# One store per 128 output rows, one DMA transposition each for q, k and exp(C), looser gates and a new instruction order in a fused Nyström attention and feed-forward kernel

## The chip, the cores and the metric

The kernel runs on one core of a Trainium2 chip. The metric is the time of one execution on the device in microseconds (us), as the median of several executions. The kernel before takes 248.0 us as the median of three runs (247.69, 248.0 and 253.92). One further execution was profiled; its own time was 247.08 us, and all durations below come from that one. The engines are called PE (TensorE, matmuls), PEld (its weight loads), DVE (VectorE), ACT (ScalarE), POOL (GpSimd) and SP (SyncE, which here only issues DMAs).

## The reference

The reference is an attention by landmarks followed by a feed-forward layer. q, k and v have 8 batches, 8 heads, 576 tokens and 64 values per head, all fp32. It is cut here to what matters:

```python
m, scale = 32, 1 / sqrt(64)
q_lm = q.reshape(B, H, 32, 18, 64).mean(axis=3)       # 32 landmarks, each the mean of 18 tokens
k_lm = k.reshape(B, H, 32, 18, 64).mean(axis=3)
A  = softmax(scale * q    @ k_lm.T)                   # 576 x 32
Bm = softmax(scale * q_lm @ k_lm.T)                   # 32 x 32
C  = softmax(scale * q_lm @ k.T)                      # 32 x 576
Z  = Bm.T / (norm_1(Bm) * norm_inf(Bm) + 1e-6)
for _ in range(6): Z = 2 * Z - Z @ Bm @ Z
x  = A @ Z @ C @ v                                    # heads side by side: 4608 x 512
h  = x @ w_in                                         # 4608 x 2048
out = (h * sigmoid(h)) @ w_out                        # 4608 x 512, fp32
```

## The kernel before, in words

The kernel works through the 8 batches, and several batches are in flight at once. The 8 heads of a batch are two groups g of four. A token has the number 18·l + j, where l is one of 32 landmarks and j one of 18 places; j is split into 9 pairs, so that j = 2·jp + c. After the transposition the two parities c lie on different halves of the partitions.

For each batch the work is this. POOL issues loads that cast to bf16 (`ld1` for k, `ld0` for q, three pieces `ldv` for v). q and k are transposed to `qT`: for batches 0 to 2 by TensorE, 128x128 at a time (`tr`, line 515, with copies `trc` behind them), for batches 3 to 7 by DMA from SP (`xt`, line 539), one DMA for each of q, k and each group g, so four of 9 blocks per batch. DVE adds the 18 places up to landmark sums (`lra` to `lrd`, line 575). PE transposes these sums (`ltr`), multiplies them (`sb`) and the rest of the chain makes Z (`ns`, `nsd`, `fb`). `A` and `C` are the two score products (each 16 tiled matmuls for both groups), `Ax` and `Cx` their exponentials on ACT, `ct` the transposition of exp(C) (by TensorE for batches 0 and 1, by DMA from SP for the others, line 814, one DMA of 6 blocks per group). `cv` multiplies exp(C) with v, `zt` with Z, and `m` with w_in, so that the first feed-forward product is done from the 128-deep `m`. DVE normalises exp(A) into `etn` (line 761), a tile of 128 partitions and 576 columns per group; its columns stand in the order c, j pair, l.

Layer 1 of a batch is 16 pieces `h` of two matmuls with 512 columns of `etn` (8 of the 9 pairs), followed by `g`, the silu on ACT (line 913), and 2 pieces `hx` of 16 matmuls with 64 columns (the ninth pair), followed by `gx`. The tokens of `hx` from four batches are collected in one tile. Layer 2 takes 256 tokens at a time by Strassen's scheme: seven products `p1` to `p7` of 8 matmuls with 256 columns, the sums `ss` on DVE before them, and copies and additions (`c`, `u`) behind them. Each 128 rows of the result lie in one of six `ost` buffers and are stored from there by four DMAs of 32 rows (`os`, line 978), from SP, at the end from SP and ACT.

The order of everything is written out by hand in one long string (`SEQUENCE`): each word is one operation, a word `*n` stands for n filler matmuls of zeros (`warm`), and `/DVE` or `/ACT` names the engine that takes a copy. Each engine executes its own words in this order, so an instruction that waits holds up all behind it on its engine. Buffers of PSUM are given out in this order too. Further dependencies are added as gates, so that transpositions and loads keep apart: a transposition `xt` of batch b waits for the second of the three v loads of its batch (line 534), the loads of batch b+1 wait for one transposition of batch b (the third in the list `xts`) and for the first `ct` of the batch before (lines 1098 to 1100), and each load waits for the eighth load before it (in `load`, line 360).

Of the kernel before, what the change touches and what calls it, by code (L numbers as in the profile page):

```python
# [8 lines left out]
BF = mybir.dt.bfloat16  # L9
# [10 lines left out]
ldk ld11.0 const ident k0cACT k0cDVE k0 *15 lms100.0 tr15.0 tr10.0 trc10.0/DVE lms106.0 lms1012.0  # L20
*6 lms110.0 lms116.0 tr114.0 lms1112.0 lmc1.0/DVE ld00.0 *6 lms000.0 tr05.0 tr00.0 trc05.0/ACT
trc114.0/ACT ltr1.0 lmT1.0/ACT trc00.0/DVE tr19.0 trc19.0/DVE trc15.0/DVE lms006.0 ld01.0
lms0012.0 lms010.0 lms016.0 lms0112.0 ld0.1 ld1.1 ldv2.0 ldv0.0 wi0b1 ldv1.0 wi0b0 tr09.0 tr014.0
lmc0.0/DVE *1 ltr0.0 lmT0.0/ACT *6 sb.0 pb.0 trc014.0/DVE trc09.0/DVE A.0 Ax01.0 Ax00.0 Ax10.0
Ax11.0 *5 C.0 Cx01.0 Cx10.0 Cx11.0 Cx00.0 pbs.0 pbr.0 bmx.0 bmt.0 csb.0 n1.0 nrm.0 tr09.1 lms000.1
lms006.1 S10.0 lms0012.1 lms010.1 bbd.0 trc09.1/DVE stz.0 f0.0 stf0.0 stf1.0 fb00.0 lms016.1
Ln10.0 S00.0 Ln00.0 fb01.0 lms0112.1 lmc0.1/DVE S01.0 ns00.0 nsd00.0 Ln01.0 S11.0 ns01.0 Ln11.0
nsd01.0 fb11.0 ctm00.0 ctc00.0/DVE tr05.1 trc05.1/ACT tr00.1 trc00.1/ACT Rs1.0 Rs0.0 ns11.0
nsd11.0 fb10.0 fb21.0 tr19.1 trc19.1/DVE ltr0.1 lms100.1 lms106.1 ns10.0 nsd10.0 lms1012.1 tr014.1
lms110.1 lms116.1 trc014.1/DVE ns21.0 tr114.1 lmT0.1/ACT wi1a wi0a wi1b1 wi1b0 wi3b0 wi3a  # L30
lms1112.1 lmc1.1/ACT tr10.1 trc10.1/ACT tr15.1 *2 ltr1.1 lmT1.1/ACT fb20.0 nsd21.0 etn1.0
trc15.1/DVE ns20.0 fb31.0 *3 ns31.0 ctm10.0 trc114.1/ACT etn0.0 nsd31.0 sb.1 pb.1 *1 A.1 Ax01.1
Ax00.1 nsd20.0 fb30.0 pbs.1 wrc.0 *1 ns30.0 nsd30.0 ctc10.0/DVE fb40.0 pbr.1 fb41.0 bmx.1 bmt.1
wi3b1 Ax11.1 Ax10.1 *5 C.1 Cx00.1 Cx11.1 Cx01.1 *1 ns40.0 nsd40.0 ns41.0 nsd41.0 fb50.0 fb51.0
cv0.0 cv1.0 wc.0 S01.1 Ln01.1 ns50.0 nsd50.0 *2 ns51.0 bbd.1 nsd51.0 zbd.0 S11.1 Ln11.1 S00.1
Ln00.1 wi2b0 wi2b1 wi2a ldv0.1 ldv1.1 *5 zt.0 ztc.0/DVE S10.1 ctm00.1 ctc00.1/DVE Rs0.1 Ln10.1
Cx10.1 *2 m1.0 mc11.0/ACT mc10.0/DVE m0.0 f0.1 mc01.0/DVE mc00.0/ACT *1 ctm10.1 ctc10.1/DVE Rs1.1
csb.1 *1 h4.0 n1.1 m3.0 nrm.1 stz.1 stf0.1 mc31.0/DVE fb00.1 g4.0 mc30.0/DVE h2.0 g2.0 h6.0 g6.0
h0.0 g0.0 h3.0 ns00.1 wrc.1 nsd00.1 fb10.1 h5.0 g5.0 m2.0 mc21.0/ACT mc20.0/DVE *1 h13.0 g13.0
ns10.1 nsd10.1 fb20.1 h15.0 hx0.0 g15.0 ns20.1 nsd20.1 fb30.1 h9.0 g9.0 h11.0 g11.0 etn0.1 ns30.1  # L40
nsd30.1 fb40.1 hx8.0 gx8.0 g3.0 h8.0 h12.0 g12.0 etn1.1 ns40.1 nsd40.1 fb50.1 gx0.0 h10.0 g10.0
ld1.2 tr15.2 trc15.2/DVE h14.0 g14.0 ns50.1 nsd50.1 zbd.1 ldv2.1 cv0.1 wc.1 tr114.2 trc114.2/DVE
tr19.2 trc19.2/DVE zt.1 g8.0 ztc.1/ACT tr10.2 trc10.2/DVE lra1.2 h7.0 g7.0 m3.1 mc31.1/ACT
mc30.1/ACT m1.1 mc11.1/DVE mc10.1/ACT h1.0 g1.0 ld0.2 tr00.2 lrb1.2 tr09.2 tr014.2 trc014.2/DVE
tr05.2 trc05.2/DVE trc09.2/DVE lrc1.2 trc00.2/ACT h12.1 g12.1 h7.1 g7.1 h15.1 m2.1 mc20.1/ACT m0.1
# [199 lines left out]
def kernel(  # L245
# [917 lines left out]
```

## Time and profile before

| what | value |
|---|---|
| median of three runs | 248.0 us |
| the profiled execution: its own time, its span from first to last instruction | 247.08 us, 245.4 us |
| mean granted TensorE clock | 0.985 |
| PE busy | 233.3 us (95% of the span) |
| PEld, DVE, ACT, POOL busy | 165.8, 180.0, 180.8, 36.7 us |
| HBM read and written | 36.70 MB, 9.44 MB |
| stores (`out_dram<-ost`) on SP and on ACT | 133 and 19 |
| DMA transpositions on SP (`qT<-qk`, `ct<-ce`) | 20 and 12 |

The span is what the engines were seen to do; 1.7 us of the execution's time lie around it. Busy shares are averages over stages that are bound by different things, so the prediction reads the stretches where PE was not busy or not at full clock, and the rows that tell what it waited for. A matmul's duration in the profile includes its way through the array, so two that follow each other overlap; what a matmul costs PE is the distance from its start to the start of the next one.

### The profile page before, as it was taken

Reading aid. Unit: us, or ns where it says so; the run is one execution under the profiler, and the core shown is the slowest. Engines: PE = TensorE matmul, PEld = TensorE weight load, DVE = VectorE, ACT = ScalarE, POOL = GpSimd, SP = SyncE. Lnnn points to the kernel's source line nnn. Section 1 sums busy time; section 2 is a strip of 40 time slices with the busy share of each in tenths; the row PEclk is TensorE's granted clock in tenths of the full one; section 3 lists DMA queues with packets and bytes.
Section 4 is the critical chain, followed back from the end, with each engine's and each line's share of the span. In section 5 each row is a group of like instructions: output and inputs, shape, how many; then the busy total and the mean of one; then the engine's idle time right before and its main releaser. Section 6 shows DMA issues by size and latency. Waiting matters only on the chain.

```text
span 245.4 us, 7471 instructions
## 1 busy us (share of the span) xinstructions
PE 233.3 (95%) x2948; PEld 165.8 (68%) x2948; DVE 180.0 (73%) x503; ACT 180.8 (74%) x432; POOL 36.7 (15%) x62
## 2 busy tenths in 40 slices
PE   7999999999999999199999999999999999999992
PEld 5986464457867556067878754777876765789882
DVE  2589889789998591489798968938899475348752
ACT  3299999988989998159746699999779788634100
POOL 8346713000050040000130060000000000000000
PEclk9999999999999999769999999999999999999999
DMA  6999999999999999793999999985414421012343
GB/s 160 207 203 197 206 207 206 210 205 204 132 177 220 202 137 178 185 194 98 136 190 171 167 185 239 190 145 136 108 47 117 121 52 39 1 43 77 88 119 109
DMA packets 55876, 36.84 MB, mean 150 GB/s; under 512 B 36640, under 2 KB 47392, under 8 KB 55840
## 3 DMA queue, kind: packets, MB, share of 16 engines
q0 software_dynamic: 15120, 18.06, 45.1%
q1 hardware_dynamic: 39808, 17.35, 34.9%
q10 hardware_dynamic: 912, 0.95, 1.4%
q8 instruction: 23, 0.38, 0.6%
q14 instruction: 13, 0.11, 0.1%
HBM read 36.70 MB, written 9.44 MB: 188 GB/s over the span
## 4 chain that ended last, share of the span: by engine, by line
PE 78%; ACT 7%; DMA 7%; SPq 3%; issue 1%; DVE 1%; ACTq 0%; DVEq 0%
PE ps L325 74%; DMA qT<-qk 6%; PE ps L515 3%; SPq L539 2%; ACT gm L913 2%; DMA gm<-in_k_dram 1%; ACT L913 1%; SPq L814 1%; ACT L1116 1%; ACT gx L936 1%; ACT m L335 1%; PE ps L802 1%; DVE red L575 1%; ACT pb L641 1%; ACT et L742 0%
## 5 line engine op out<-in xcount | busy, mean ns | idle before, releaser
L913 ACT ACTIVATE gm<-ps 128x512 f16<-128x512 f32 x128 | 68.7, 621 | 15.0 <-PE ps L325 14.3
L325 PE MATMUL ps<-etn,m 128*128 128x512 bf16 (+1 forms) x512 | 73.5, 289 | 0.2
L325 PEld LDWEIGHTS <-gm 128*128 128x128 f16 x512 | 48.6, 98 | 12.5 <-issue 1.3
L325 PE MATMUL ps<-w_out_sb,gm 128*128 128x256 f16 (+1 forms) x392 | 53.0, 281 | 0.0
L325 PEld LDWEIGHTS <-ss 128*128 128x128 f16 x408 | 39.5, 99 | 9.8 <-issue 1.8
L325 PEld LDWEIGHTS <-m 128*128 128x128 bf16 x512 | 31.5, 98 | 20.8 <-issue 3.2
L325 PE MATMUL ps<-wt,ss 128*128 128x256 f16 x272 | 35.5, 276 | 0.2
L1036 DVE TENSOR_TENSOR ost<-ost,ps 128x256 f32<-128x256 f32 x51 | 20.9, 416 | 13.4 <-PE ps L325 7.4
L335 ACT COPY ost<-ps 128x256 f32<-128x256 f32 (+1 forms) x45 | 17.2, 388 | 10.9 <-PE ps L325 10.6
L335 ACT CAST m<-ps 128x512 bf16<-128x512 f32 x36 | 19.4, 612 | 1.1 <-PE ps L325 0.8
L337 DVE CAST m<-ps 128x512 bf16<-128x512 f32 x28 | 18.3, 685 | 2.3 <-PE ps L325 1.9
L710 DVE SCALAR_TENSOR_TENSOR st<-st,ps 128x128 bf16<-128x128 bf16 (+2 forms) x54 | 13.6, 257 | 8.5 <-PE ps L325 5.5
L407 POOL DMA_DIRECT2D v<-in_v_dram x24 | 14.0, 590 | 30.8 <-DMA qT<-qk 13.6
L325 PE MATMUL ps<-w_out_sb,ss 128*128 128x256 f16 x136 | 17.5, 273 | 0.0
L325 PE MATMUL ps<-wt,gm 128*128 128x256 f16 x120 | 15.5, 272 | 0.0
L575 DVE TENSOR_TENSOR red<-qT 128x1024 f16<-128x1024 bf16 x12 | 8.3, 689 | 9.4 <-DMA qT<-qk 9.2
L685 DVE TENSOR_TENSOR fb<-st,hmask 128x256 bf16<-128x256 bf16 (+1 forms) x54 | 14.4, 271 | 0.8
L752 ACT ACTIVATE ln<-ps 128x288 f32<-128x288 f32 x32 | 12.4, 423 | 2.7 <-PE ps L325 2.4
L787 ACT ACTIVATE ce<-ps 128x288 bf16<-128x288 f32 x32 | 13.0, 424 | 1.7 <-PE ps L325 1.6
L1001 DVE TENSOR_TENSOR ss<-gm 128x1024 f16<-128x1024 f16 x15 | 10.2, 686 | 5.2 <-ACT gm L913 5.2
L742 ACT ACTIVATE et<-ps 128x288 bf16<-128x288 f32 x32 | 11.1, 423 | 3.6 <-PE ps L325 3.6
L337 DVE COPY ost<-ps 128x256 f32<-128x256 f32 x25 | 10.5, 420 | 3.2 <-PE ps L325 3.0
(93 smaller groups left out, 332.0 us busy)
## 6 DMA issues: line engine op xcount, KB each, us to landing
out_dram<-ost SPq DMA_DIRECT2D x126, 64.0 KB, 2.1
v<-in_v_dram POOLq DMA_DIRECT2D x24, 192.0 KB, 10.0
qk<-in_q_dram POOLq DMA_DIRECT2D x7, 576.0 KB, 10.6
qk<-in_k_dram POOLq DMA_DIRECT2D x7, 576.0 KB, 9.2
w_out_sb<-in_moe_w_out_dram POOLq DMA_DIRECT2D x4, 512.0 KB, 15.1
w_in_sb<-in_moe_w_in_dram POOLq DMA_DIRECT2D x8, 128.0 KB, 7.2
w_in_sb<-in_moe_w_in_dram POOLq DMA_DIRECT2D x4, 256.0 KB, 9.0
out_dram<-ost ACTq DMA_DIRECT2D x10, 64.0 KB, 1.7
```

The source lines that it names most:

```text
L325: nc.tensor.matmul(out=out_ap, lhsT=lhsT, rhs=rhs, start=start, stop=stop, skip_group_check=True)
L335: nc.scalar.copy(out=out, in_=in_)
L337: nc.vector.tensor_copy(out=out, in_=in_)
L407: lambda e, a=a: nc.gpsimd.dma_start(out=v_r[b % 2][a * L:(a + 1) * L, :, :], in_=v[b].rearrange("h (l a x) d -> a l h (x d)", l=L, a=VA)[ ...
L575: lambda e: nc.vector.tensor_tensor(out=o_, in0=a_, in1=b_, op=OP.add),
L685: nc.vector.tensor_tensor(out=fb[it % 2][:, g0:g1], in0=bc(sr[it % 3][:, g0:g1, 0:L], 4, 2), in1=bc(hmask, n, 1), op=OP.mult), [o], 14.5 + ...
L710: nc.vector.scalar_tensor_tensor(out=s2[:, g0:g1, lo:SW], in0=s[:, g0:g1, lo:SW], scalar=2.0, in1=ps[:, 0:NG * SW].rearrange("p (g x) -> p ...
L742: lambda e, g=g, et=et, c=c: nc.scalar.activation(out=et[:, c], in_=bank(me["A"], 2 * g + c)[:, 0:HS], func=AF.Exp, scale=sc / J),
L752: lambda e, g=g, c=c, ln=ln: nc.scalar.activation(out=ln[:, c], in_=bank(me["S", g, c])[:, 0:HS], func=AF.Ln),
L787: nc.scalar.activation(out=ce[:, :, 0:VP].rearrange("p (i c) (a l) -> p c a i l", c=2, a=VA)[:, c], in_=bank(me["C"], 2 * g + c)[:, 0:HS]. ...
L913: lambda e, dc=dc, cell=cell: nc.scalar.activation(out=gm[:, dc, :], in_=bank(cell["o"]), func=AF.Silu),
L1036: nc.vector.tensor_tensor(out=out_, in0=x, in1=y, op=OP.add)
```

## The change

The change touches the order and the layout of the columns of `etn`, and with it the tokens that a store writes.

- `etn` is written in the order c, l, j pair instead of c, j pair, l. The instruction still runs over j and then l, so its output steps by 9 elements (18 bytes) from one element to the next. `h` reads runs of 8 elements with one left out between runs. `hx` reads the ninth element of each run, with the two halves c next to each other in its order: neighbours in its stream lie 288 elements apart.
- By that, 128 result rows are 16 landmarks times 8 places of one parity, and one DMA stores them. The last pair goes out as 64 rows per batch.
- q and k are transposed by one DMA of 18 blocks each (not one per group), exp(C) by one of 12 blocks.
- Gates: a transposition waits for the first v load, not the second; the loads of the next batch wait for the first transposition in the list; the dependency on the eighth load before is dropped from the plan (the eight semaphores of the POOL queue still make an eighth load wait); three of the four preparations of w_out for Strassen's scheme and the first silus lose a dependency.
- `A` and `C` are two operations each, one per group, with two PSUM banks each instead of four.
- The order string is another one throughout, with 84 fillers instead of 64 and, on ACT, 13 changes of the activation table after the first instead of 11.

Batches 0 to 2 are transposed by TensorE in both versions; what is new is where these transpositions stand in the order.

```diff
 SEQUENCE = """
-ldk ld11.0 const ident k0cACT k0cDVE k0 *15 lms100.0 tr15.0 tr10.0 trc10.0/DVE lms106.0 lms1012.0
+const ldk ld11.0 ident ld00.0 ld01.0 ld0.1 k0cDVE k0cACT ld1.1 fold k0 *18 lms100.0 lms106.0
...
-ce_r = ring(smp, [128, VI, 128], BF, "ce", 2)
-ct_r = ring(smp, [128, VI, 128], BF, "ct", 2)
+ce_t = smp.tile([128, NG, VI, 128], BF, tag="ce", name="ce")
+ct_t = smp.tile([128, NG, VI, 128], BF, tag="ct", name="ct")
+ce_r, ct_r = [ce_t[:, g] for g in range(NG)], [ct_t[:, g] for g in range(NG)]
...
     def load(name, prio, us, issue, emit, deps=(), after=()):
         d = list(deps) + list(after)
-        if len(swdge) >= 8:
-            d.append((swdge[-8], None))
...
-            gate = v_ops[b][-2:-1]
+            gate = v_ops[b][:1]
             for t in (1, 0):
-                for g in range(NG):
-                    qt_ops[t, g] = [A(
-                        f"xt{t}{g}.{b}", [("SP", 1.38)],
-                        lambda e, t=t, g=g: nc.sync.dma_start_transpose(
-                            out=qT[:, t, g], in_=qk[:, t, g].rearrange("p j d -> p (j d)")),
-                        [qk_ops[b, t, g]] + use + gate, p0 + 5, lag=XLAG)]
...
+                o = A(f"xt{t}.{b}", [("SP", 1.8)],
+                      lambda e, t=t: nc.sync.dma_start_transpose(
+                          out=qT[:, t].rearrange("p g j x -> p (g j) x"),
+                          in_=qk[:, t].rearrange("p g j d -> p (g j d)")),
+                      [qk_ops[b, t, g] for g in range(NG)] + use + gate, p0 + 5, lag=XLAG)
...
             def etm(e, g=g, et=et, ln=ln):
-                nc.vector.tensor_tensor(out=etn[:, g, :], in0=et.rearrange("p c x -> p (c x)"),
-                                        in1=ln.rearrange("p c x -> p (c x)"), op=OP.mult)
+                nc.vector.tensor_tensor(
+                    out=etn[:, g, :].rearrange("p (c l j) -> p c j l", c=2, l=L),
+                    in0=et.rearrange("p c (j l) -> p c j l", l=L),
+                    in1=ln.rearrange("p c (j l) -> p c j l", l=L), op=OP.mult)
...
-                ct_ops[g] = [A(f"ct{g}.{b}", [("SP", 1.38)], lambda e, ce=ce, ct=ct:
...
+                after = v_ops.get(b + 1, [])[:1]
+                ct_ops[0] = ct_ops[1] = me["cts"] = [A(
+                    f"ct0.{b}", [("SP", 1.5)], lambda e: nc.sync.dma_start_transpose(
+                        out=ct_t.rearrange("p g i x -> p (g i) x"),
+                        in_=ce_t.rearrange("p g i x -> p (g i x)")),
+                    me["csum", 0] + me["csum", 1] + [prev.get("cv")] + after, p0 + 20, lag=XLAG)]
...
             def hm(e, dc=dc, cell=cell):
                 ps = bank(cell["o"])
                 for g in range(NG):
-                    mm(ps.rearrange("p (c x) -> p c x", c=2),
-                       m_sb[:, g, dc * 128:(dc + 1) * 128], etc[:, g, :, 0:256],
+                    mm(ps.rearrange("p (c l j) -> p c l j", c=2, l=L),
+                       m_sb[:, g, dc * 128:(dc + 1) * 128], etc[:, g, :, :, 0:JP - 1],
                        start=(g == 0), stop=(g == 1))
...
                         for g in range(NG):
-                            mm(ps[:, d].rearrange("p (c x) -> p c x", c=2),
+                            mm(ps[:, d].rearrange("p (l c) -> p l c", c=2),
                                m_sb[:, g, (d0 + d) * 128:(d0 + d + 1) * 128],
-                               etc[:, g, :, 256:288], start=(g == 0), stop=(g == 1))
+                               etc[:, g, :, :, JP - 1].rearrange("p c l -> p l c"),
+                               start=(g == 0), stop=(g == 1))
...
-    def store(e, t, place, m, cols=slice(0, DMODEL)):
-        b, j = place[m]
-        {"SP": nc.sync, "ACT": nc.scalar}[e].dma_start(
-            out=out[b * S:(b + 1) * S, cols].rearrange("(l j) n -> j l n", j=J)[j],
-            in_=t[L * m:L * m + L, cols])
+    def store(e, t, place, cols=slice(0, DMODEL)):
+        b, c, h = place
+        q = {"SP": nc.sync, "ACT": nc.scalar}[e]
+        if h is not None:
+            return q.dma_start(out=out[b * S:(b + 1) * S, cols].rearrange(
+                "(l j c) n -> c l j n", c=2, j=JP)[c, L // 2 * h:L // 2 * (h + 1), 0:JP - 1],
+                in_=t[:, cols])
+        r = [q.dma_start(out=out[x * S:(x + 1) * S, cols].rearrange(
+            "(l j) n -> l j n", j=J)[:, J - 2:J], in_=t[64 * n:64 * n + 64, cols])
+            for n, x in enumerate((b, b + 1)) if c is None or n == c]
+        return r[0]
...
     def later_loads(b):
         p = last[b - 2]
-        gate = last[b - 1].get("xts", [])[-2:-1]
+        gate = last[b - 1].get("xts", [])[:1]
         if b - 2 >= NCT:
             gate = gate + last[b - 2]["cts"][:1]
```

More of the change, by code (lines that the diff above doesn't have):

```diff
@@ L26 @@
[L26 to L31, printed above, removed]
@@ L502, in attn @@
         qt_ops = {}
-        use = [prev2[x] for x in ("A", "C") if x in prev2]
+        use = [prev2[x, g] for x in "AC" for g in range(NG) if (x, g) in prev2]
         if on_pe:
@@ L742, in attn @@
                       lambda e, g=g, et=et, c=c: nc.scalar.activation(
-                          out=et[:, c], in_=bank(me["A"], 2 * g + c)[:, 0:HS], func=AF.Exp,
+                          out=et[:, c], in_=bank(me["A", g], c)[:, 0:HS], func=AF.Exp,
                           scale=sc / J),
-                      [me["A"], prev.get(f"etn{g}")], p0 + 21 + g, table="exp",
-                      group=grp).reads(me["A"], 2 * g + c)
+                      [me["A", g], prev.get(f"etn{g}")], p0 + 21 + g, table="exp",
+                      group=grp).reads(me["A", g], c)
                 me["S", g, c] = A(f"S{g}{c}.{b}", [("PE", mm_us(HS))],
@@ L914, in layer1 @@
                                    out=gm[:, dc, :], in_=bank(cell["o"]), func=AF.Silu),
-                               [o] + ([last[1]["pb"]] if not b else []), p,
+                               [o], p,
                                table="silu").reads(o))
```

329 lines of the change are left out of this document (167 added, 162 removed).

## The prediction

> **What bounds the kernel now.** I read the slices of the page first, then the windows of ten microseconds, the chain of waits, and the order of matmuls around the one hole.
>
> ```profile
> PE   7999999999999999199999999999999999999992
> ...
> PEclk9999999999999999769999999999999999999999
> DMA  6999999999999999793999999985414421012343
> ```
>
> PE is busy in all but one inner slice, the 17th (98 to 104 us), and just there the granted clock falls. So the end is set by the sum of PE's work plus this hole, the start and the tail. The windows give its size.
>
> ```profile
> 90.00:100.00 10.00, 8.75 (x77) 5.18 (x74) 2.94 (x5) 8.31 (x17) 0.00 (x0) 1.00 1.21 168
> 100.00:110.00 10.00, 5.83 (x29) 3.54 (x30) 7.58 (x18) 2.75 (x7) 0.00 (x0) 0.66 0.87 189
> 110.00:120.00 10.00, 10.00 (x121) 8.21 (x120) 8.27 (x28) 8.53 (x30) 0.71 (x1) 1.00 0.63 100
> ```
>
> After the window's length the columns are PE, PEld, DVE, ACT and POOL busy, the clock, the DMA share and GB/s. All engines starve together while DMA stays busy: they wait for a transfer. The chain of waits (start, length, what) names it.
>
> ```profile
> 86.72 14.41 DMA qT<-qk
> ...
> 101.23 0.70 DVE red L575
> ...
> 104.17 15.06 PE ps L325 x139
> ```
>
> The last of four transpositions of batch 4 took 14.4 us. The median is 4.2:
>
> ```profile
> L539 SPq DMA_TRANSPOSE qT<-qk x20: 1301/1405/4201, 52.3 to 163.9; - x20
> ...
> DMA to landing us min/median/max: 3.3/4.2/14.4
> ```
>
> On POOL's queue, 0.4 us before it, begins a row of four loads for batch 5 (86.34 to 88.9). The transposition shared the DMA engines with them. PE's own lines give the cost:
>
> ```profile
> 98.12 0.63 PE L325 MATMUL ps<-etn,m 128*128 128x64 bf16 x16
> 104.17 0.39 PE L325 MATMUL ps<-rs,fold 128*128 128x256 f16 x1 [5.42 <-DVE rs L575]
> 104.36 2.77 PE L325 MATMUL ps<-etn,m 128*128 128x512 bf16 x6
> 106.92 1.75 PE L325 MATMUL ps<-wt,ss 128*128 128x256 f16 x8
> 108.50 1.04 PE L325 MATMUL ps<-w_out_sb,ss 128*128 128x256 f16 x8
> ```
>
> PE stands for 5.42 us and then runs at half clock: six `h` matmuls in 2.56 us from start to start where they else take six times 0.216, 1.30 (+1.26); eight product matmuls in 1.58 where the next eight take 0.87 (+0.71). **The hole costs 5.42 + 1.26 + 0.71 = 7.4 us.**
>
> **The change, part by part.** The sum is made on the profiled execution, 247.08 us.
>
> *The hole, −7.4 us.* I counted PE's work along the new order by the spacing of these rows (`h` 0.432, a product 0.872, `hx` 0.466, `A` and `C` together 0.37 each, a filler 0.11). Between the place of a q transposition and the `ltr` that needs it stand 10.5, 12.9, 10.9, 9.4 and 11.6 us for batches 3 to 7. A block of 18 is not in the trace. Nine blocks occupy SP 1.33 us undisturbed (5.63 us for the four from 159.67) and six 1.21: 0.04 a block over about 1 us, so an estimated 1.7 us for 18. Its landing I bound below by the 3.3 us of nine blocks and above by two in a row, 5.6 us; I take 5 us, nearest to the pair, since the bytes are the pair's. With 1.7 us of landmark additions (0.69 + 0.42 + 0.29 + 0.29) that is 6.7 us, inside all five distances. The longest wait seen, 14.4, would not fit: that is a rival. SP spends 10 × 1.7 + 6 × 1.45 = 26 us in place of 20 × 1.33 + 12 × 1.21 = 41 us; SP is on the path only through the transpositions, so this counts nothing by itself.
>
> *Stores, 0.* 152 become 48. The stores' queue time (0.42 us each) lies beside PE; two stores fewer stand behind the last copy.
>
> *Tail, −0.8 us.* The last copy starts at 240.99 and takes 0.42, so ends at 241.4; the last of 19 stores on ACT starts at 242.42, as the queues are still full. In the new order two stores follow the last copy, one on SP and one on ACT, so the last starts about 1 us sooner; each is twice as large, for which I give 0.2 back. Bounds: 0 and −1.
>
> *Fillers, +2.2 us.* 20 more at 0.11 us, full clock:
>
> ```profile
> 6.46 0.82 PE L325 MATMUL ps<-zer 128*128 128x256 bf16 x6
> ```
>
> They stand in the first 31 us of PE's work. Where they only fill a wait they cost nothing, so the bounds are 0 and +2.2. I take 2.2, since PE had next to no idle in 10 to 60 us before.
>
> *Loads of the start, +0.7 us.* Loads land one after the other at a full rate (about 2.9 us for a batch of q or k, 1.0 for a piece of v, 0.6 and 1.4 for pieces of w_in) until about 58 us. The new order brings batch 2's q and k ahead of w_in and of most of v. Counted by these steps from batch 1's k (landed at 15.6), the last piece for `m0.0` lands at about 29.8, while PE reaches it at about 29.1 (25.1 us of its work plus 4 us of lag, as before at that place). The other places have the data by 0 to 2 us. Bounds: 0 and +3.
>
> *The layout of `etn`.* No instruction of the trace steps by 18 bytes or more from element to element, neither in writing (DVE) nor as moving operand of PE. These are the unknowns:
>
> ```profile
> L325 PE MATMUL ps<-etn,m 128*128 128x512 bf16 x256 | 66.0, 385 | 0.2
> ...
> L325 PE MATMUL ps<-etn,m 128*128 128x64 bf16 x256 | 9.6, 193 | 0.0
> ...
> L761 DVE TENSOR_TENSOR etn<-et,ln 128x576 bf16<-128x576 bf16 x16 | 12.0, 751 | 0.2 <-ACT ln L756 0.2
> ```
>
> `etn` lies between 0.75 us and, at two passes for each of 576 elements, 1.35 us. The DVE queue has room on average (180 of 245 us), but behind `etn` stand additions that free PSUM, and in batches 1, 2, 3, 5 and 7 the first `h` follows the second `etn` within 1 to 2.5 us of PE's work. I take 0.3 us in these five, **+1.5 us**; ends 0 and +6 (two times 0.6 us in five batches). A faster write is excluded: the step only adds hops. The Trainium skill ("Vector Engine (DVE) Microarchitecture Reference", 5.2 Measured stream behaviour on trn2) states 1.71 to 2.5 ns a column where the output hops at every element, against 1.05. By an estimate from these figures `etn` would take 1.1 to 1.6 us; no run here shows such a write.
>
> `h` leaves out one element in nine: I count 0. `hx` steps far at every element: its 256 matmuls come every 0.029 us ((0.63 − 0.193) / 15 from the line at 98.12), which is hardly more than 64 columns at full clock. At one column per two clocks, as seen in the half-clock rows, it would be 0.053. Bounds 0 and far above; I take 0, nearest to the row itself, and make the rest a rival.
>
> *The rest, 0.* Two more table loads of 1.28 us fall on ACT, which has 65 us idle. Split `A` and `C` issue the same matmuls. Dropped dependencies only let things start earlier; what a load now meets earlier is in the rivals.
>
> **Sum:** 247.1 − 7.4 − 0.8 + 2.2 + 0.7 + 1.5 = **243.3 us** on the profiled execution. The two undisturbed runs shown lie 0.6 and 0.9 us above it (247.69 and 248.0), so I forecast **244.0 us**, 4 us below 248.0, with an own range of 240.3 to 246.3: below it lie all fillers and the layout at nothing, above it loads and DVE at half their upper ends.
>
> **Rivals.**
>
> *`hx` at half rate.* 256 × 0.024 = 6.2 us of PE work that nothing hides, since PE is the bound: about 250. For it: 64 columns that each lie 576 or 18 bytes from the one before, at a spacing that leaves no slack. Against: no row shows that PE's reads slow down. The Trainium skill ("SBUF — State Buffer", Door 1: The DMA port swizzle, the note on SBUF cachelines) says that accesses are at full bandwidth while at least two fall into one line of 16 bytes; eight bf16 elements may be stepped over free of charge, and `hx` steps further. By it `hx` would be slow and `h` not. Chance 0.20.
>
> *`hx` much slower: the change ends slower than before.* The same place, a larger price. The gain without it, 4 us, is eaten at 0.029 + 4/256 = 0.045 us per matmul; 2% slower than 248 it is from 0.029 + 9/256 = 0.064 us. At four clocks a column (0.107) it adds 20 us: 264. For it: the spacing shows what one access per clock gives and nothing of one line per access. Chance 0.12.
>
> *A new collision in place of the old.* The loads of batch 5 now wait for the first transposition of batch 4 and the third batch's exp(C). These are issued about 4 us ahead of the q transposition, so the loads start while that is in flight. If it then takes 14.4 us as before, it and its additions need 16.1 us where 12.9 stand: a stall of 3.2 us, plus 1 to 2 at half clock, and likewise in one further batch: 248 to 252. Against it: only two loads meet it, and they drain in some 6 us. Chance 0.10.
>
> *DVE becomes the bound.* `etn` at its upper end or above it, with additions and the silus' sums queued behind it: +4.5 to +9 over the forecast, 248.5 to 253. For it: DVE is busy 0.83 to 0.98 of most windows from 110 to 190 us. Chance 0.08.
>
> That the change doesn't do all it says is so in one part: batch 2 is transposed by TensorE already before (both issue the same 24 blocks of `tr`, and the first DMA transposition is batch 3's). It gives nothing, and nothing is counted for it.
>
> **Chances and range.** Forecast 0.50, the others 0.20, 0.12, 0.10 and 0.08. Two per cent of 248.0 (243.0 and 253.0) is about what a measurement of this kernel can tell from no change. The forecast's point lies 1 us above 243.0, so of its 0.50 I give 0.33 to faster and 0.17 to within. Half-rate `hx`, the collision and most of the DVE case lie within: 0.17 + 0.18 + 0.10 + 0.06 = 0.51. Slower: 0.12 + 0.02 + 0.02 = 0.16. The range of 8 in 10 goes from 240.3 to 253.
>
> **What would show it.** Right: no stretch of low clock near 100 us, and no wait of PE for `rs` above 1 us; the 64-column group at 9.6 us busy with a spacing of 0.029; SP with 16 transpositions of 1.5 to 1.7 us; `etn` at 0.75 to 1.1 us. Wrong: a mean spacing of the 64-column matmuls of 0.05 or more, `etn` above 1.3 us with PE waiting for DVE, a transposition landing after 10 us, or PE waiting for w_in in the first 40 us by more than 3 us.

## The result and the profile after

| | before | after |
|---|---|---|
| median | 250.0 us (4 runs, 247.69 to 253.92) | 298.6 us (4 runs, 296.16 to 300.99) |
| ratio | 1 | 1.201, 95% interval 1.186 to 1.216 |
| profiled execution: time, span | 247.08, 245.4 us | 296.16, 294.5 us |
| mean granted TensorE clock | 0.985 | 0.993 |
| PE, DVE, ACT busy | 233.3, 180.0, 180.8 us | 265.9, 210.0, 188.8 us |

The change made the kernel 20% slower. The forecast was 244.0 us, within 240.3 to 253.0: wrong by 54.6 us and on the other side.

The slices and the chain of the page after (40 slices of the span; then the shares of the chain that ended last):

```profile
PE   6986979899998899969998799899977969999994
...
PEclk9999799999999999999999999999999999999999
DMA  7999999926998991997569499900325400002144
...
PE 70%; DVE 20%; DMA 4%; issue 3%; ACT 1%; POOL 1%; DVEq 0%; POOLq 0%; ACTq 0%
PE ps L323 69%; DVE etn L757 11%; DMA qk<-in_k_dram 4%; DVE m L335 2%; DVE st L706 1%; DVE fb L681 1%; DVE ost L1044 1%; DVE ss L1009 1%; PE ps L511 1%; POOL qk L390 1%; ACT pb L637 1%; DVE qT L335 1%; DVE ost L335 0%; ACT gm L914 0%; DVE pbs L657 0%
```

The deep hole near 100 us with its low clock has gone, as forecast; one short dip of the clock stands near 33 us. In place of the hole PE has a little idle time nearly everywhere, and DVE, which held 1% of the chain before, holds 20%, more than half of it with one line: `etn`. The groups by shape show that instruction and its two readers (count | busy us, mean ns of one | idle before and its releasers):

```profile
L323 PE MATMUL ps<-etn,m 128*128 128x512 bf16 x256 | 70.3, 406 | 6.6 <-DVE m L335 4.3 <-DVE etn L757 2.1
...
L757 DVE TENSOR_TENSOR etn<-et,ln 128x576 bf16<-128x576 bf16 x16 | 43.2, 2702 | 0.0
...
L323 PE MATMUL ps<-etn,m 128*128 128x64 bf16 x256 | 32.3, 293 | 0.0
```

`etn` takes 2.70 us where it took 0.75: 16 times 1.95, 31.2 us more on DVE. A piece `hx` (16 matmuls of 64 columns) takes PE 1.850 us from start to start where it took 0.466: 16 times 1.385, **22.2 us** more. A piece `h` takes 0.485 in place of 0.432: 128 times 0.053, **6.8 us** more. The spacing of the 64-column matmuls, which the prediction named first among the signs of being wrong, is 0.116 us, beyond even the 0.107 of its slower-side rival.

How 2.7 us on DVE become idle time on PE is seen in the chain of waits of after, at 215 us (start, length, what):

```profile
214.00 2.15 PE ps L323 x21
...
216.22 0.42 DVE ost L1044
216.65 2.61 DVE etn L757
219.26 0.13 DVE st L706
...
219.41 0.29 DVE fb L681
219.70 0.33 DVE ost L1044
```

And the timeline of the same stretch, with PE's idle time and its releaser in brackets:

```profile
219.76 0.23 PE L323 MATMUL ps<-st,fb 128*128 128x64 bf16 x2 [1.70 <-DVE fb L681]
```

`h` does not wait here. Behind `etn` on DVE stand `st` and `fb`, the short steps of the next batch's Z, and additions that free PSUM; PE's next product in the chain of Z needs `fb` and stands 1.70 us for it. This is why only 2.1 us of PE's idle time carry the name of `etn`: the instructions queued behind it are the releasers. The largest waits of PE by releaser (us in total, times, longest):

```profile
PE ps L323 <- DVE m L335: 5.9, 4, 1.7
PE ps L323 <- DVE fb L681: 5.0, 3, 1.7
PE ps L323 <- DVE etn L757: 2.1, 2, 1.1
PE ps L323 <- DVE st L706: 2.0, 2, 1.0
```

`m` at line 335 is the copy of the product `m` out of PSUM, on DVE as well.

The transpositions of q and k on SP (instruction time in ns, then landing in us):

```profile
L533 SPq DMA_TRANSPOSE qT<-qk x10: 2694/3570/4955, 68.6 to 186.8; - x10
...
DMA to landing us min/median/max: 5.2/5.9/8.9
```

A block of 18 holds SP for at least 2.69 us, which is twice the 1.33 of nine blocks; the prediction had 1.7. It lands after 5.9 us (forecast 5), and the longest landing is 8.9 us, where it was 14.4.

### The profile page after: what moved, and what is told of

Its sections match the earlier page's. It is cut to its first block, busy times and chain, and to the rows that moved or that the text cites. A ratio compares the mean times of both kernels' runs of the same rounds, so it can differ in the third digit from the quotient of the medians.

```text
span 294.5 us, 7298 instructions
## 1 busy us (share of the span) xinstructions
PE 265.9 (90%) x2968; PEld 189.2 (64%) x2968; DVE 210.0 (71%) x498; ACT 188.8 (64%) x439; POOL 36.7 (12%) x62
## 4 chain that ended last, share of the span: by engine, by line
PE 70%; DVE 20%; DMA 4%; issue 3%; ACT 1%; POOL 1%; DVEq 0%; POOLq 0%; ACTq 0%
PE ps L323 69%; DVE etn L757 11%; DMA qk<-in_k_dram 4%; DVE m L335 2%; DVE st L706 1%; DVE fb L681 1%; DVE ost L1044 1%; DVE ss L1009 1%; PE ps L511 1%; POOL qk L390 1%; ACT pb L637 1%; DVE qT L335 1%; DVE ost L335 0%; ACT gm L914 0%; DVE pbs L657 0%
## 5 line engine op out<-in xcount | busy, mean ns | idle before, releaser
L323 PE MATMUL ps<-etn,m 128*128 128x64 bf16 (+1 forms) x512 | 100.0, 350 | 6.6 <-DVE m L335 4.3
L323 PEld LDWEIGHTS <-m 128*128 128x128 bf16 x512 | 52.1, 106 | 34.6 <-issue 7.9
L757 DVE TENSOR_TENSOR etn<-et,ln 128x576 bf16<-128x576 bf16 x16 | 43.2, 2702 | 0.0
L333 ACT COPY ost<-ps 128x256 f32<-128x256 f32 x52 | 18.6, 376 | 21.1 <-PE ps L323 17.7
L706 DVE SCALAR_TENSOR_TENSOR st<-st,ps 128x128 bf16<-128x128 bf16 (+2 forms) x54 | 15.0, 283 | 21.6 <-PE ps L323 15.0
L335 DVE CAST m<-ps 128x512 bf16<-128x512 f32 x35 | 24.4, 712 | 2.5 <-PE ps L323 2.3
L333 ACT CAST m<-ps 128x512 bf16<-128x512 f32 x29 | 16.2, 589 | 5.2 <-PE ps L323 3.8
L938 ACT ACTIVATE gx<-ps 128x512 f16<-128x512 f32 x16 | 9.7, 605 | 11.8 <-PE ps L323 11.8
L323 PEld LDWEIGHTS <-fb 128*128 128x128 bf16 x96 | 8.8, 100 | 12.5 <-DVE fb L681 6.7
L1009 DVE TENSOR_TENSOR ss<-gm 128x1024 f16<-128x1024 f16 x15 | 10.3, 686 | 8.2 <-ACT gm L914 8.2
L323 PE MATMUL ps<-st,fb 128*128 128x64 bf16 (+1 forms) x96 | 11.3, 194 | 5.0 <-DVE fb L681 5.0
```

Of the source, the lines that this page charges most:

```text
L323: nc.tensor.matmul(out=out_ap, lhsT=lhsT, rhs=rhs, start=start, stop=stop, skip_group_check=True)
L333: nc.scalar.copy(out=out, in_=in_)
L335: nc.vector.tensor_copy(out=out, in_=in_)
L706: nc.vector.scalar_tensor_tensor(out=s2[:, g0:g1, lo:SW], in0=s[:, g0:g1, lo:SW], scalar=2.0, in1=ps[:, 0:NG * SW].rearrange("p (g x) -> p ...
L757: nc.vector.tensor_tensor(out=etn[:, g, :].rearrange("p (c l j) -> p c j l", c=2, l=L), in0=et.rearrange("p c (j l) -> p c j l", l=L), in1 ...
L938: lambda e, d0=d0, cell=cell, c=c: nc.scalar.activation(out=gx[:, d0:d0 + 8, c:c + 64], in_=bank(cell["o"]).rearrange("p (c x) -> p c x", ...
```

## The experiments

My theory after the result: the layout of `etn`'s columns carries the whole loss (its write, and the steps at which `hx` and `h` read it), and the rest of the change gains a few us. The rival: the order, the gates or the transpositions cost much by themselves.

### The layout taken back, four stores per 128 rows

```diff
-                nc.vector.tensor_tensor(
-                    out=etn[:, g, :].rearrange("p (c l j) -> p c j l", c=2, l=L),
...
+                nc.vector.tensor_tensor(out=etn[:, g, :], in0=et.rearrange("p c x -> p (c x)"),
...
-                       m_sb[:, g, dc * 128:(dc + 1) * 128], etc[:, g, :, :, 0:JP - 1],
+                       m_sb[:, g, dc * 128:(dc + 1) * 128], etx[:, g, :, 0:256],
...
-                               etc[:, g, :, :, JP - 1].rearrange("p c l -> p l c"),
+                               etx[:, g, :, 256:288], start=(g == 0), stop=(g == 1))
...
+        for m, (b, j) in enumerate(place):
+            {"SP": nc.sync, "ACT": nc.scalar}[e].dma_start(
+                out=out[b * S:(b + 1) * S, cols].rearrange("(l j) n -> j l n", j=J)[j],
+                in_=t[L * m:L * m + L, cols])
```

The last four lines take the place of the single store; `etx` is the same tile with its columns as c, x.

> The changed kernel with its new order, gates, one-piece transpositions and fillers, but with the layout of etn as before: etn written contiguously, h and hx reading contiguous runs, and each 128 rows of the result stored by four DMAs of 32 rows again. Layout theory: the whole loss is in the layout, and the rest of the change is worth what the prediction gave it (7.4 us of the hole and 0.8 of the tail gained, at most 2.2 + 0.7 us lost): 241 to 246 us, against 250 for the kernel before in the same job. Rival, the order: the new order, gates or transpositions cost much by themselves: above 255 us. etn should be back at 0.75 us, hx at 0.47 us and h at 0.43 us from start to start.

Measured: 264.2 us (263.5 to 266.2), 1.065 times the kernel before (1.057 to 1.073). `etn`, `hx` and `h` are back at 0.75, 0.466 and 0.432 us, yet the time lies 18 us above what the theory gave. SP's instructions in this run between 110 and 125 us tell of a cost that this experiment brought in itself:

```profile
110.27 1.72 SPq L978 DMA_DIRECT2D out_dram<-ost  x4
112.16 3.30 SPq L533 DMA_TRANSPOSE qT<-qk  x1
115.50 3.87 SPq L978 DMA_DIRECT2D out_dram<-ost  x8
119.48 2.70 SPq L533 DMA_TRANSPOSE qT<-qk  x1
122.28 2.78 SPq L978 DMA_DIRECT2D out_dram<-ost  x4
```

The new order has one store at each of these places; with four, eight stores hold SP for 3.87 us ahead of a transposition, and PE stands 3.4 us behind `hx8.3`, at the end of the chain from that transposition and its sums. Another one (issued at 91.35) landed after 10.3 us, and the `ltr` that needs it came 5.8 us late. The clock adds to it: in the profiled execution, granted 0.964, 12.0 us of PE's busy time lie in stretches at half clock (granted 0.5), so about 6 us are lost there. So the run could not separate order from stores, and one that leaves the stores alone was needed.

### One part back at a time

The first takes back only the write, the second only `hx`, the third only `h`, each by its lines of the diff above.

> The changed kernel with only the write of etn contiguous again (columns c, j, l); h and hx still read at the new steps, so they multiply other tokens than the stores name: the assignment of result rows to tokens is changed, the amount of work is not. Layout theory: etn falls from 2.70 to 0.75 us, the waits of PE for DVE behind it (about 26 us) go, the dearer h (6.7 us) and hx (22.2 us) stay: 267 to 275 us. Rival, that DVE's slow write hides beside PE and the matmuls are everything: 290 us or more.

> The changed kernel with only hx reading contiguous runs again (two runs of 32 columns per group); it then multiplies other tokens than the stores name, with the same amount of work. Layout theory: the 16 pieces hx fall from 1.85 to 0.47 us, 22.2 us less PE work; part of it may turn into waits for etn, which DVE still writes in 2.7 us: 273 to 282 us. Rival, that the wait for DVE takes the place of all of it: 290 us or more.

> The changed kernel with only h reading 2 x 256 contiguous columns again (other tokens than the stores name, the same amount of work). Layout theory: h falls from 0.485 to 0.432 us, 128 times 0.053 = 6.7 us less PE work, part of which may turn into waits for etn: 289 to 295 us. Rival, that the 9/8 in h comes from the waits around it and not from the runs of 8 with one left out: h stays at 0.485 us and the time at 296.

Measured, one execution each: 274.2, 276.6 and 299.7 us, beside 296.2 of the changed kernel's profiled execution. The first two lie where the theory had them, and their rivals fall. Of the write's 31.2 us on DVE, 22.0 us were on the path. The group lines of the run with the contiguous write:

```profile
L323 PE MATMUL ps<-etn,m 128*128 128x512 bf16 x256 | 70.0, 408 | 0.2 <-DVE m L335 0.2
...
L323 PE MATMUL ps<-etn,m 128*128 128x64 bf16 x256 | 32.3, 293 | 0.0
...
L757 DVE TENSOR_TENSOR etn<-et,ln 128x576 bf16<-128x576 bf16 x16 | 12.0, 748 | 0.0
```

The matmuls are as dear as in the changed kernel, but the idle time before them is 0.2 us in place of 6.6, and PE is busy 97% of the span. The third run missed. `h` did fall to 0.432 us, so the 9/8 is in the reading, but the time did not fall with it. PE's waits before the same matmuls are only a little longer (7.1 us in place of 6.6):

```profile
L323 PE MATMUL ps<-etn,m 128*128 128x512 bf16 x256 | 67.6, 397 | 7.1 <-DVE m L335 4.8 <-DVE etn L757 2.2
```

What differs is the granted clock, 0.960 in this execution and 0.993 in that of the changed kernel. By slices of the span:

```profile
PEclk9999799999999999957999599999999999799999
```

Four stretches stand at half clock, where the changed kernel has one, and 22.2 us of PE's busy time lie in them in place of 3.4. There an `h` matmul comes every 0.426 us in place of 0.216, so half of that time is lost: about 11 us in place of 2. The 9 us between are more than the 6.8 that the reading gives back, and PE's idle time in all grows by only 2 (30.4 us in place of 28.5). So the run does not show that the saving turned into waits. Whether the faster `h` brings on the stretches at half clock, one execution cannot tell; the changed kernel itself ran 299.3 and 301.0 us in executions with a clock of 0.971. The price of `h` is thus known as PE's work, and as time only together with that of `hx` (below).

### One store with the old layout, and the layout in the old order

A store of 128 rows does not need the new layout: its address can run over 4 places and then 32 landmarks.

```diff
-                "(l j c) n -> c l j n", c=2, j=JP)[c, L // 2 * h:L // 2 * (h + 1), 0:JP - 1],
+                "(l j c) n -> c j l n", c=2, j=JP)[c, 4 * h:4 * h + 4],
```

> The changed kernel with etn, h and hx as before (columns c, j pair, l, all contiguous), and still one store per 128 rows: the store's three-step address simply runs over 4 places and then 32 landmarks, so the new layout is not needed for it. Order, gates, one-piece transpositions and fillers are those of the changed kernel. Theory A: the layout carries the whole loss, and the 264 us of the run with 152 stores came from four stores of 0.42 us at each place of SP's queue that the order had given to one, with the transpositions behind them: 241 to 247 us. Theory B: order, gates or the one-piece transpositions cost by themselves: 256 us or more.

> The kernel before, in its old order and with its 152 stores, with only the columns of etn in the order c, l, j pair (the write, the reads of h and hx, and the rows that each store of 32 names). Theory A: 22.2 us for hx and 6.7 us for h are added on PE, and 31 us on DVE, of which a part becomes waits: 280 to 305 us, the loss of the whole change from this part alone. Theory B: the layout costs what the new order could not hide, and the old order hides more of it: below 275 us.

Measured: 311.2 us (304.0 to 314.4) and 308.8 us. Neither theory had the cause of the first, though its time lies within the second theory's "256 us or more". Its chain of waits at 155 us:

```profile
155.71 1.28 DMA out_dram<-ost
156.99 11.04 DMA qT<-qk
168.04 11.07 DMA ct<-ce
```

SP's instructions in the same stretch:

```profile
155.71 1.17 SPq L980 DMA_DIRECT2D out_dram<-ost  x2
156.99 9.03 SPq L533 DMA_TRANSPOSE qT<-qk  x1
166.12 0.54 SPq L980 DMA_DIRECT2D out_dram<-ost  x1
166.75 1.18 SPq L982 DMA_DIRECT2D out_dram<-ost  x2
168.04 7.13 SPq L813 DMA_TRANSPOSE ct<-ce  x1
```

The transposition behind two such stores holds SP for 9.0 us and lands after 11; all of these places together make 22% of the chain for transpositions and 6% for stores. Six of the 16 transpositions land after 9 to 12 us. Issuing a store takes SP 0.54 us; what holds the queue is the transfers. The order and the bytes are those of a run shown below (246 us), only the shape of the store differs: 4 places times 32 landmarks here, 16 landmarks times 8 places there. The Trainium skill ("DMA: Bandwidth & Descriptors", Why a DMA increments its semaphore by 16 and not by 1) says that a DMA is spread over the largest number of engines, up to 16, that divides the slowest dimension of both sides: 4 here and 16 there. The trace agrees: a store of 128 rows here gets one update of its semaphore about 1 us after its issue and then four from its data, in all 36 of them, where each of the 48 stores of the other run gets 16. Where the queue is otherwise empty, such a store here takes 5.7 to 5.9 us to land, there 2.8. So the shape of the store is shown to be the cause of this loss, and the trace shows that such a store lands in four parts in place of 16. That a transposition waits until these parts are through is read from the times alone.

The second run looks from the other side: the layout alone, in the old order with its 152 stores, costs 61.7 us over the profiled execution of the kernel before; its 308.8 us are somewhat more than my 280 to 305. Some 9 us of this are the clock (0.950): 22.7 us of PE's busy time lie at half clock, where the kernel before has 4.2. The 52 us that are left stand beside 50.1 in the new order (296.2 against 246.1, below). The old order hides no more of the layout than the new. Its groups by shape have nearly the same durations as those of the changed kernel:

```profile
L325 PE MATMUL ps<-etn,m 128*128 128x512 bf16 x256 | 74.1, 417 | 1.5 <-DVE etn L761 1.2 <-DVE m L337 0.2
...
L325 PE MATMUL ps<-etn,m 128*128 128x64 bf16 x256 | 31.9, 293 | 0.0
```

### A table of prices

On the kernel of the single stores every `hx`, `h` and `etn` got an address pattern of its own (`e2` is the `etn` tile of both groups as one row):

```diff
+                                src = e2[:, 0:64 * s].rearrange("p (n s) -> p n s", s=s)[:, :, 0]
...
+                    src = e2[:, 0:512 // r * s].rearrange("p (n s) -> p n s", s=s)[:, :, 0:r]
...
+                sp = lambda x: x.rearrange("p (a s) -> p s a", s=s)
```

The first line is `hx` at step s, the second `h` with r columns of every s, the third `etn` at step s.

> A table of prices, not a comparison of times: the kernel with the single stores, in which each of the 16 hx, the 16 values of dc of h and the 16 etn uses another address pattern (so the columns are other tokens; the amount of work is the same). hx: 64 columns at steps of 1 to 10, 12, 16 and 18 elements, the pattern of the change, pairs at 18, fours at 36. h: runs of 512, 256, 128, 64, 32, 16, 8, 4, 2 and 1 columns with gaps. etn: output steps of 2 to 64 elements, and input steps of 2 to 32 with a contiguous output. Theory A (PE pays for every element that it passes over, up to a limit): step 2 costs 2 clocks a column, 3 costs 3, 4 costs 4, from 5 on 4.33; h pays 9/8 for every pattern with one left out in nine, and 2 for 8 of 16. Theory B (PE pays per run): runs of 8 cost 9/8 whatever the gap, of 16 17/16, of 4 5/4, of 2 3/2. Theory C (PE pays by lines of 16 bytes): steps up to 4 cost nothing or little, and the price jumps at step 8. For etn, A: the price of 4.5 to 4.7 ns an element is reached from some step between 2 and 9 on and stays there; B: it grows with the step up to 64; and a strided input costs less than 1.5 us, or as much as a strided output.

Measured, worked out from the starts of the matmuls (medians at full clock) and the durations of `etn` in its trace, where each pattern of `hx` and `etn` occurs once:

```
hx: us per matmul of 64 columns
step         1      2      3      4      5      6      7      8      9      12     16     18
us         0.029  0.029  0.046  0.060  0.073  0.087  0.101  0.116  0.120  0.115  0.118  0.116
pairs at step 18: 0.060   fours at step 36: 0.029   the change's pattern: 0.113

h: us per matmul of 512 columns (r columns of every s)
512 of 512, 256/288, 64/72, 16/18, 8/10, 8/16: 0.216      8/12: 0.220   32/33: 0.222
4/8: 0.226   1/2: 0.227   16/17: 0.229   8/9: 0.242   4/5: 0.242   2/3: 0.243

etn: us for 576 elements, the output at step s
step         2      3      4      6      8      9      16     32     64
us         0.816  1.097  1.437  2.091  2.715  2.693  2.610  2.674  2.726
both inputs at step s, output contiguous: 2: 0.748   4: 1.179   8: 1.209   16: 1.204   32: 1.198
```

For `hx` the price rises in proportion to the step from 2 to 8 elements and then stays. Eight bf16 elements are 16 bytes: the 64 columns touch 8·s lines of 16 bytes for a step s up to 8, and 64 lines beyond. Divided so, every step from 3 on costs 1.80 to 1.92 ns a line, and a step of 2 (16 lines) costs no more than a step of 1, 0.029 us. The pairs and fours agree (32 lines, 0.060; 16 lines, 0.029). So PE gets one line in 1.8 ns, a little over the time of four columns (0.42 ns each in `h`), and needs four columns from each. Read by steps, this is theory A's form with another slope (half a clock for each element passed over, up to 4.3 clocks a column); theory B falls, and C has the unit right and the threshold wrong.

For `etn` the same division gives 4.7 to 5.1 ns a line of output for steps 3 to 8, and the price stays from 8 on. At steps of 4 or more, the two inputs cost 2.1 ns an element, less than half of a strided output.

For `h` the price is of another kind: an odd step between runs costs one clock for each run, at most one for each 8 columns (8/9, 4/5 and 2/3 alike), while an even one costs nothing, 2% (8/12) or 5% (4/8, 1/2). The numbers show the rule of odd steps; why 8 of 12 costs 2% they leave open. 4/8 and 1/2 touch 128 lines, and 128 times 1.81 ns is 0.232 us, near their 0.226 and 0.227.

The Trainium skill ("SBUF — State Buffer", Door 1, the note on SBUF cachelines), which the prediction weighed, has the line of 16 bytes right. Its condition, two accesses to a line, is too weak here: step 4 has two and costs PE 2.1 times and DVE's output 1.9 times. The Trainium skill ("Vector Engine (DVE) Microarchitecture Reference", 5.2 Measured stream behaviour on trn2), whose figures are for streams of 32-bit words, led me to an estimate of 1.1 to 1.6 us for `etn`; 2.70 was measured.

### The hole by itself

```diff
-nsd40.3 ct0.3 xt00.4 ld1.5 ldv0.4 h9.2 g9.2 g14.2 h1.2 h0.2 g1.2 g0.2 cv0.3 ldv1.5 fb50.3
+nsd40.3 ct0.3 xt00.4 xt11.4 xt01.4 xt10.4 ld1.5 ldv0.4 h9.2 g9.2 g14.2 h1.2 h0.2 g1.2 g0.2 cv0.3 ldv1.5 fb50.3
...
-        gate = last[b - 1].get("xts", [])[-2:-1]
+        xts = last[b - 1].get("xts", [])
+        gate = xts[:1] if b == 5 else xts[-2:-1]
```

The three words that are new in the first line are taken from their old place behind `ss00@5220.0`.

> The kernel before with one thing moved: the last three transpositions of batch 4 stand directly behind the first in the order, and the loads of batch 5 wait for the last of the four instead of the third in the list. No engine's own order changes. If the 7.4 us of the hole are what the profile shows (a transposition of 14.4 us beside the loads), the hole goes: 239 to 243 us, with no low clock near 100 us. Rival: the loads of batch 5, about 4 us later, are missed at the next transpositions, and the hole only moves on: 246 us or more.

Measured: 245.8 us, 0.988 of the kernel before (0.977 to 0.998); the profiled execution 244.96, 2.1 us below that of before. The transposition that had taken 14.4 us lands after 4.7, and PE runs through that place. But batch 5's loads now start at 92.4 us in place of 86.3, its own transpositions at 101.3, and PE stands there. The chain of waits:

```profile
102.64 0.31 SPq L538
...
103.00 3.45 DMA qT<-qk
...
106.57 0.70 DVE red L574
```

The windows around it (columns as in the prediction):

```profile
100.00:110.00 10.00, 6.93 (x73) 5.38 (x72) 4.82 (x15) 6.14 (x15) 0.00 (x0) 0.99 1.05 194
110.00:120.00 10.00, 9.91 (x92) 7.57 (x91) 6.80 (x24) 7.33 (x27) 0.71 (x1) 0.84 0.80 132
```

`p2` takes 4.11 us in place of 0.87, and two products behind it run at half clock (0.81 and 0.91 more): 5.0 of the 7.4 us come back. Expectation and rival each had a half of it: the collision was real and is gone, and the next batch's data is late by the time that the loads were kept back.

### The rest of the change by itself

The changed kernel with the old layout and its own stores untouched:

> The changed kernel with etn, h and hx contiguous as before and with the stores exactly as the changed kernel issues them (16 landmarks times 8 places, 48 DMAs). The rows so stored are not the tokens that the addresses name: only the assignment of rows to tokens is changed, not the work. Theory A (the layout carries the loss; the 311 us of the single store over 4 places came from that store, whose outermost dimension has 4 steps, and not from the order): from the run with the contiguous write alone, 274.2 - 22.2 (hx) - 6.7 (h) = 245 us; 242 to 248. Theory B (the order, the gates or the one-piece transpositions cost by themselves): above 256.

Measured: 246.5 us (245.2 to 247.1), 0.985 of the kernel before (0.978 to 0.992). The profiled execution has 246.10 us. That decides between the theories, and makes the sum close:

| step, on profiled executions | us |
|---|---|
| the changed kernel | 296.2 |
| its write contiguous | −22.0 → 274.2 |
| its reads contiguous too (22.2 + 6.8 = 29.0 by the spacings) | −28.1 → 246.1 |
| the kernel before | 247.1 |

### Three ways to keep one store

The next lets the silu reorder the columns while it reads PSUM, the one after moves the steps from `etn`'s output to its inputs:

```diff
-                                   out=gm[:, dc, :], in_=bank(cell["o"]), func=AF.Silu),
+                                   out=gm[:, dc, :].rearrange("p (c l j) -> p c l j", c=2, l=L),
+                                   in_=bank(cell["o"]).rearrange("p (c j l) -> p c l j", c=2, l=L),
+                                   func=AF.Silu),
```

```diff
+                    out=etn[:, g, 0:512].rearrange("p (c l j) -> p c l j", c=2, l=L),
+                    in0=et4[:, :, :, 0:JP - 1], in1=ln4[:, :, :, 0:JP - 1], op=OP.mult)
+                nc.vector.tensor_tensor(
+                    out=etn[:, g, 512:576].rearrange("p (l c) -> p l c", c=2),
```

The third puts the silu's reordering and the moved transpositions into the old order.

> The same, but with the right tokens: the silu g reads its PSUM bank in the order c, l, j (steps of 32 elements) and writes gm contiguously, gx likewise, so that 128 result rows are 16 landmarks times 8 places and one DMA stores them. If ACT reads PSUM at steps for nothing, the 128 g stay at 0.62 us and the time is that of the run before it in this job, 242 to 248 us. Rival: PSUM read at steps costs what the strided SBUF access cost (2 ns an element or more): g takes 1.1 us or more, ACT becomes the bound with some 250 us of work, and the time is above 265.

> The changed kernel with the steps moved from etn's output to its inputs: etn is written contiguously in the order c, l, 8 places, and behind that 64 columns l, c of the ninth; h and hx read contiguous columns; stores as in the changed kernel, all tokens right. By the table of prices, a strided input costs 2.1 ns an element, so etn takes about 1.1 + 0.2 us in two instructions in place of 2.7, PE has no extra work: 243 to 252 us (0.5 us of DVE 16 times, of which at most half becomes waits). Rival: DVE is so near to the bound that all of it comes back: above 254.

> The old order with what the runs showed to pay: the transpositions of batch 4 moved as before, the loads of batch 5 waiting for the third of the four (it landed at 90.9, the last at 91.9 us), the v load of batch 4 behind the loads of batch 5 on POOL (so the piece that the next transposition waits for lands about 1 us sooner), and one store per 128 rows with the silu reading PSUM in the order c, l, j; the stores of the last batch stay 64 KB each, now of 128 columns. Theory: the run with the moved transpositions was 4.4 us below the kernel before and kept 3.2 us of waiting and some 1.7 us at half clock at batch 5; 2 us earlier loads take about 2 us of that, the stores' queue is shorter: 241 to 245 us, against 250 for the kernel before in the same job. Rival: that wait hangs on the transfers themselves, and the time is that of the moved transpositions alone, 245.8 or more.

Measured: the silu version takes 247.1 us, 0.982 of before (0.971 to 0.994). A `g`, with PSUM read at steps of 32 elements (durations in ns, minimum, median and maximum):

```profile
L913 ACT ACTIVATE gm<-ps x128: 592/618/806, 35.1 to 221.2; 128x512 f16<-128x512 f32 x128
```

The run of the order alone, with contiguous reads, has 618 ns in the median too, so the reordering is free there. With the steps on `etn`'s inputs, 248.9 us, 1.003 of before (0.998 to 1.008): `etn` takes 1.06 + 0.22 us as expected, and the 0.54 us more, 16 times, cost 2.4 us in all (248.49 against 246.10 in the profiled executions). The groups of `etn`:

```profile
L758 DVE TENSOR_TENSOR etn<-et,ln 128x512 bf16<-128x512 bf16 x16 | 17.0, 1064 | 0.0
...
L761 DVE TENSOR_TENSOR etn<-et,ln 128x64 bf16<-128x64 bf16 x16 | 3.6, 223 | 0.0
```

The old order with moved transpositions and reordering silu takes 246.5 us, 0.995 of before (0.990 to 0.999). The wait at batch 5 stays (3.7 us in place of 5.0, again `p2` and two products behind it), as its rival said: the first transposition is issued 2.5 us sooner (98.8), but beside the last loads it lands after 5.75 us in place of 3.85. So no version here is shown to be better than the kernel before by more than 2%; the silu version has the lowest ratio of those that store the right tokens, and its interval overlaps that of the moved transpositions.

## Why the prediction was wrong

**`etn`: "I take 0.3 us in these five, +1.5 us; ends 0 and +6"** is the first step that failed. The upper end, two passes for each element, was a guess at a mechanism and no bound: nothing in the trace excluded more. The write took 3.6 times its old time and put 22.0 us on the path. The counting by five batches was too narrow as well. It looked at the `h` that waits for `etn`; most of PE's waits for DVE are for the copies of `m` (5.9 us) and the Z steps `fb` and `st` (7.0 us) queued behind it, and 15 of the 16 `etn` stand in the chain of waits. With the contiguous write the waits for `fb`, `st` and `etn` are gone and 0.2 us remain for `m`. The rival that DVE becomes the bound had this mechanism, at 4.5 to 9 us and a chance of 0.08.

**`hx`: "Bounds 0 and far above; I take 0, nearest to the row itself"** is the second. The nearest row was one of contiguous reads, and what it could tell of strided ones was nothing. The slower-side rival had the place, the mechanism (a line fetched for each column) and nearly the price: 20 us at 0.107, measured 22.2 at 0.116. It had a chance of 0.12, and half rate had 0.20. An open price that is paid 256 times on the engine that sets the end should have drawn the forecast, or at least the range, towards it; the range stopped at 253.

**`h`: "I count 0"** failed too, by 6.8 us of PE's work. It was not given a bound at all. A slip beside it made no difference: the columns of `hx` do not lie "576 or 18 bytes" apart but 576 forward and 558 back in turn, and the table has 0.113 us for this pattern beside 0.116 for a plain step of 18 elements.

**The rest of the sum** can be checked against the run of the order alone. Without the layout the sum was 241.8 us; that run's execution took 246.1. I gave each operation of PE the price that it has undisturbed, and took what it needed beyond that, by stretch:

| PE's time beyond its work, us | before | order alone | forecast of the difference |
|---|---|---|---|
| 0 to 60 (loads) | 6.6 | 9.5 | +0.7, bounds 0 to +3 |
| 60 to 90 | 2.0 | 1.0 | 0 |
| 90 to 110 (the hole) | 7.6 | 2.2 | −7.4 |
| 110 to 130 | 1.2 | 0.8 | 0 |
| 130 to 150 | 1.2 | 3.7 | 0 |
| from 150 on | 2.7 | 1.7 | 0 |
| PE's work itself | 218.4 | 220.1 | +2.2 (fillers) |
| from PE's end to the span's end | 4.45 | 4.14 | −0.8 |

*Loads:* +2.9, at the upper bound: `m0.0` stands behind 23.5 us of work and starts at 32.2, a lag of 8.7 us where I had counted 4 and before had 5.6. But no wait of PE for w_in stands in this stretch. What stands there is 0.91 us for k (at 7.37) and 1.23 us for q (at 14.53), beside one wait of 0.49 before: the loads that come first were late, not those that the sum looked at. The rest of the 2.9 has no such row. *The hole:* the mechanism was right, and 5.4 of 7.4 us came. The rest is a new wait at the very place, named in the chain of waits of that run together with one of the same kind in batch 6 (130 to 150):

```profile
89.23 7.28 DMA qT<-qk
133.17 6.84 DMA qT<-qk
```

They are the collision rival in a small form: 1.1 and 1.7 us at the two `ltr` behind them, not 4 to 8. *The size of a transposition* (2.7 us on SP in place of 1.7) is a term that was mis-sized; it may have its part in these two, which no run separates. *Fillers:* the work grew by 1.7, near the 2.2. *Tail:* 0.3 us in place of 0.8. Small gains elsewhere, 2.4 us in all, were not forecast. With all of it, what I took for a gain of 5 us (247.1 to 241.8) is one of 1.

## What to carry to other kernels

A step of 16 bytes or more between elements is an open price until a row shows one like it, on DVE's side and on PE's. Multiply it out over all instructions that would pay it, and if the product can eat the gain, let the forecast follow the product. Where data must change its order, look for the place where the step is free: here it cost 22 us at DVE's output, 28 us at PE's reads, about 2.4 us at DVE's inputs and nothing where ACT reads PSUM. To price a slower instruction, look at what is queued behind it on its engine, not only at its readers.

## What was not expected of the hardware

PE's moving operand comes at one line of 16 bytes in 1.8 ns, so fewer than four bf16 columns from a line cost time; at DVE's output it is 4.7 ns a line or a little more. Runs of up to 8 columns with an odd step between them cost PE one eighth more. A DMA store of 128 rows with 4 steps in its outermost dimension held transpositions behind it to 9 to 12 us, and the same bytes with 16 steps did not (7.3 us at the longest). A transposition of 18 blocks holds its queue at least as long as two of nine (2.69 us against 2 times 1.33), so joining them saved SP nothing.
